# A pre-norm block with dilated local attention and an MLP: Wo's loads, a K halo and sums of h in another order, and seven products for all 18 pairs of W2 rows in group 5

## The chip, the cores and the metric

The kernel runs on one core of one Trainium2 chip. The metric is the device time of one execution in microseconds. Five engines run side by side, each in the order of its own instructions: TensorE (PE; its weight loads are shown as PEld), VectorE (DVE), ScalarE (ACT), GpSimd (POOL) and the SyncE queue (SP), which issues most of the DMAs.

## The reference

```python
h  = x + A(layernorm(x))        # x: 2048 rows of 576, bf16
h2 = h + B(layernorm(h))

def A(x):                       # 32 heads of 18, window 8, dilation 2
    q, k, v = split(x @ wqkv)   # wqkv: 576 x 1728
    idx = pos[:, None] - arange(8) * 2
    logits = einsum("bhsd,bhswd->bhsw", q, k[idx]) * 18 ** -0.5   # masked where idx < 0
    return einsum("bhsw,bhswd->bhsd", softmax(logits), v[idx]) @ wo

def B(x):
    y = layernorm(x)
    return gelu(y @ w1 + b1) @ w2 + b2      # w1: 576 x 4608, w2: 4608 x 576
```

## The kernel before

**Tiles and order.** The 2048 rows are 16 tiles of 128; tile j holds the rows 16 p + j, one per partition p. So the window of a row lies in the tiles j, j-2, ... of the same parity, and where it goes below tile 0 it comes from the partition before. K and V of the eight tiles of one parity lie in `kv_ring[j % 2]`. When a tile has been done, its own slot is loaded again from `kv_dram`, one partition shifted (`halo(j, 1)` for K, `halo(j, 2)` for V), for the tiles that follow. The attention goes through the tiles in `ATT_ORDER`, even ones from 14 down, then odd ones from 15 down, and the MLP in `GROUPS` of two: group 0 is tiles 14 and 12, group 4 is 15 and 13, group 5 is 11 and 9, group 6 is 7 and 5, group 7 is 3 and 1. All orders are written out by hand: each engine, the SP and POOL queues included, runs its instructions in the order of the program text.

**The QKV stage** has 24 visits of PE (two products of one tile each), with lists of what follows each visit: `after` for the other engines and `loads` for weight loads. A weight load is tied to the last evacuation before it (`pace`). The normed x of the odd tiles is turned by DMA: `out_x(i)` stores two tiles, `in_x(i)` reads them back transposed; `in_x(0)` serves the products from visit 12, `in_x(1)` those from visit 15, `in_x(2)` those from visit 18. `load_wo(qs)` issues two DMAs for each of four parts of Wo. Wo is first used in visit 17.

**The group stage.** For group k the loop runs MLP1 (four visits, v = 0 to 3; lists `m1[v]` are called ahead of each), in which ACT writes gelu into `h_all`, 36 blocks of F for the group's two tiles; after the visits 0 to 2 its first 24 blocks are there. Then comes MLP2 (`mlp2_fast` from group 2 on), and ahead of its products the visit of Wo for the two tiles c, d of group k+1. During this time DVE does the attention of the tiles e, f of group k+2 (`att_qk_one` is product, halo, sums; then `att_max`, `exps` on ACT, `att_den`), and in the next group's `m1[0]` `pv_sum` of both with `send_o` and `read_o`, which store o and read it back transposed into oT for Wo.

**Seven products.** In `mlp2_fast` two tiles of tokens, two blocks of F (a pair of W2 rows) and two halves of the columns make a 2 x 2 block product. 18 pairs m make up F. For pairs below `rows` it is done with seven products (`PRODUCTS`), which need four sums of h (`h_sums`, t = 0 to 3; s_slot gives their place) and four of W2 (`w2_sums`, t_slot; made once and kept). The pairs from `rows` on are done plainly with eight (`plain`). `rows` is 16 in the groups 2 to 5 and 18 in the groups of `FULL`, 6 and 7. Sum t=2 of h and t=2 of W2 are made in place, over a block that the seven products don't need. The sums of the pairs 0 to 11 lie in `kv_ring[0]`, those of 12 to 15 in rows of `q_all` or `x_all` that are free at that time. The hooks `x["hc"]`, `x["h"]`, `x["7"]`, `x["exp"]` and so on are called between the products, in the order of the list `steps`; h(c) and h(d) in the text are `ln2_h`, which adds Wo's product pw to x. `out1` ("o1") on DVE adds up the second tile's results, `reload_x` fetches x again for a later group, `out_sum` and `accumulate_hs` are DMAs of POOL that add into `x_all`.

Of the kernel before, what the change touches and what calls it, by code (L numbers as in the profile page):

```python
# [11 lines left out]
BF16 = mybir.dt.bfloat16  # L12
F32 = mybir.dt.float32
F16 = mybir.dt.float16
# [3 lines left out]
def kernel(  # L18
# [13 lines left out]
    P = 128  # L32
# [6 lines left out]
    KT = 5  # L39
# [5 lines left out]
    HALF = D // 2  # L45
# [10 lines left out]
    GROUPS = [ATT_ORDER[i:i + 2] for i in range(0, NT, 2)]  # L56
# [551 lines left out]
    def ring_blocks(r, b0, n, size):  # L608
        flat = kv_ring[r][:].rearrange("p w t d -> p (w t d)").bitcast(F16)
        return flat[:, b0:b0 + n * size].rearrange("p (m c) -> p m c", c=size)  # L610
# [5 lines left out]
    def t_slot(t, m0, m1):  # L616
        if t == 2:
            return w2_block(0, 1, m0, m1).bitcast(F16)
        i = (0, 1, None, 2)[t]
        if m0 >= 16:  # L620
            return ring_blocks(1, (2 * i + m0 - 16) * HALF, m1 - m0, HALF)
        if i == 2 and m0 < 16:
            return ring_blocks(0, RING_T + m0 * HALF, m1 - m0, HALF)
        part = 0 if m1 <= 8 else 1 if m1 <= 12 else 2
        rows, j0 = ((x_all, (1, 9, 13)[part]), (q_all, (4, 12, 0)[part]))[i]
        m = m0 - (0, 8, 12)[part]
        j = j0 + 2 * (m // 2)
        if m1 - m0 > 2:
            return rows[:, j:j + m1 - m0 - 1:2, :].bitcast(F16).rearrange("p a (b c) -> p a b c", c=HALF)
        return rows[:, j, (m % 2) * HALF:(m % 2 + m1 - m0) * HALF].bitcast(F16).rearrange("p (b c) -> p b c", c=HALF)  # L630

    SR = 12
    ring1_free = [False]
    step_of = [0]
    RING_T = 3 * SR * P

    def s_slot(t, m0, m1):
        if t == 2:
            return h_block(0, 1, m0, m1)
        i = (0, 1, None, 2)[t]  # L640
        if m0 < SR:
            return ring_blocks(0, (i * SR + m0) * P, m1 - m0, P)
        if not ring1_free[0]:
            rows, j = ((q_all, 15), (x_all, 10), (x_all, 8))[i] if step_of[0] == 2 else (q_all, 15 - 2 * i)
            return rows[:, j, (m0 - SR) * P:(m1 - SR) * P].bitcast(F16).rearrange("p (m c) -> p m c", c=P)
        return ring_blocks(1, 6 * HALF + (i * (NM - SR) + m0 - SR) * P, m1 - m0, P)

    def h_block(odd, i, m0, m1):
        return h_all[:, 2 * m0 + odd:2 * m1:2, i * P:(i + 1) * P].bitcast(F16)
# [49 lines left out]
    def c_(fn, *a):  # L699
        return lambda: fn(*a)  # L700
# [2 lines left out]
        return ap.rearrange("p (g c) -> p g c", g=2)  # L703

    def mlp2_fast(g, rows, tags, wo, hooks):
        last, summed = wo is None, rows < NM
        q, p, r, s = tags
        j0, j1 = g
        af = psum_pair(q, "po")
        a, f = (af[:, n, 0:HALF] for n in range(2))  # L710
        b, d = psum_pair(p, "po")[:, 0, 0:HALF], None
        o0, o1 = (new_o(j, summed) for j in g)
        flat = kv_ring[1][:].rearrange("p w t d -> p (w t d)")
        rest = halves(flat[:, W * 2 * D - 2 * D:W * 2 * D].bitcast(F32))
        bank = {1: a, 2: a, 3: f, 4: b, 6: b}

        def add(out, x, y):
            nc.vector.tensor_tensor(out=out, in0=x, in1=y, op=ALU.add)

        def last_out():  # L720
            nc.vector.tensor_copy(out=o0[:, HALF:HALF + HALF // 2], in_=f[:, 0:HALF // 2])
            nc.scalar.copy(out=o0[:, HALF + HALF // 2:D], in_=f[:, HALF // 2:HALF])
            nc.sync.dma_start(out=out3[:, j0, HALF:D], in_=o0[:, HALF:D])

        def out0(n0, n1):
            if summed:
                nc.scalar.copy(out=halves(o0), in_=af[:, :, 0:HALF])
                return
            add(halves(o0)[:, n0:n1], af[:, n0:n1, 0:HALF], halves(x_of(j0))[:, n0:n1])
            nc.sync.dma_start(out=out3[:, j0, n0 * HALF:n1 * HALF], in_=o0[:, n0 * HALF:n1 * HALF])  # L730

        def out1():
            if summed:
                add(o1[:, HALF:D], bank[5], o1[:, 0:HALF])
                add(o1[:, 0:HALF], b, o1[:, 0:HALF])
                out_sum(j1)
                return
            add(o1[:, 0:HALF], b, rest[:, 0])
            add(o1[:, HALF:D], bank[5], rest[:, 1])
            nc.sync.dma_start(out=out3[:, j1, :], in_=o1)  # L740

        def do_rest():
            if summed:
                nc.scalar.copy(out=o1[:, 0:HALF], in_=bank[7])
                return
            add(rest, bank[7].unsqueeze(1).to_broadcast([P, 2, HALF]), halves(x_of(j1)))

        def take():
            bank[7], bank[5] = (psum_pair(tag, "po")[:, 0, 0:HALF] for tag in (r, s))

        lo, hi, all_ = (0, SR), (SR, rows), (0, rows)
        seed = {"b": (1, 6), "d": (6, 5), "f": (5, 3)}
        does = {
            "wo": lambda: wo((r, s)), "e": take, "rest": do_rest, "o1": out1,
            "o0": lambda: last_out() if last else out0(0, 2), "lo": lambda: out0(0, 1),
            "11": lambda: plain(0, 0, a, rows), "12": lambda: plain(0, 1, f, rows),
            "21": lambda: plain(1, 0, b, rows), "22": lambda: plain(1, 1, bank[5], rows),
        }
        if rows < NM:
            steps = ["wo", "hc", (1, all_), "b", "h", "e", (7, lo), (2, all_), (6, all_), "6", "7", "d", "11", (7, hi), "rest", "in",  # L760
                      (5, all_), "f", "exp", (4, all_), "21", "22", "o1", "4", (3, all_), "12", "o0", "3"]
        elif not last:
            steps = ["wo", "hc", (1, all_), "b", "h", "e", (7, lo), (6, all_), "6", "d", "7", (2, all_), (7, hi), "rest", "in",
                     (5, all_), "f", (4, all_), "o1", "4", (3, all_), "o0"]
        else:
            steps = ["e", (1, lo), (7, lo), (1, hi), "b", "h", (7, hi), "rest", (6, all_), "d", (2, all_), "lo",
                     (5, all_), "f", (4, all_), "o1", (3, all_), "o0"]
        for step in steps:
            if isinstance(step, tuple):
                product(step[0], bank[step[0]], *step[1])  # L770
            elif step == "f" and last:
                add(f, bank[5], x_of(j0)[:, HALF:D])
            elif step in seed:
                nc.scalar.copy(out=bank[seed[step][1]], in_=bank[seed[step][0]])
            else:
                call([does[step]] if step in does else hooks.get(step, ()))
# [22 lines left out]
    with tc.manual_schedule(engines={ENG.PE, ENG.Activation, ENG.DVE, ENG.SP, ENG.Pool}):  # L799
# [129 lines left out]
            ln2_ins(c, d)  # L929

        loads = {}
        for v, fns in ((2, [(load_w1, 0)]), (3, [(load_w1, 1)]), (4, [(load_w1, 2)]), (6, [(load_wo, [0])]), (8, [(load_wo, [1, 2])]),
                       (11, [(load_wo, [3])]), (14, [(load_w1, 4)]), (18, [(load_w1, 5), (load_w2, 0)]), (19, [(load_w2, 1)]),
                       (20, [(load_w2, 2)]), (21, [(load_w2, 3)]), (22, [(load_w2, 4)])):
            loads[v] = [c_(*fn) for fn in fns]
        after = {
# [87 lines left out]
        def wo_visit(*duos, fill=False):  # L1024
            visit([wo_duo(j, tag) for j, tag in duos], (lambda: [ahead[0]() for _ in range(2)]) if fill else None)

        FULL = (6, 7)
        p, q, r, s = "ABDC"

        gelu_table()  # L1030
        for k, g in enumerate(GROUPS):
# [38 lines left out]
            if 2 < k < 7:  # L1070
                m1[0] += [c_(pv_sum, c), c_(send_o, c), c_(pv_sum, d), c_(read_o, c), c_(send_o, d), c_(read_o, d)]
            if k < 6:
                m1[1] = m1.get(1, []) + [c_(att_qk_one, e, 0)]
                m1.setdefault(3, [])
                if k == 2:
                    m1[0] += [c_(pv_sum, d), c_(send_o, d), c_(read_o, d)]
                    m1[3] += [c_(w2_sums, 0, 8, (2, 3)), c_(w2_sums, 8, 12, (2, 3)), c_(w2_sums, 12, 14, (0, 1)), c_(w2_sums, 14, 16, (0, 1)),
                              c_(w2_sums, 12, 14, (2, 3)), c_(w2_sums, 14, 16, (2, 3))]
                m1[3] += [c_(h_sums, 0, SR, (0,))]
                x["hc"] += [c_(h_sums, 0, SR, (2,))]  # L1080
                x["h"] += [c_(h_sums, 0, SR, (1, 3)), c_(h_sums, SR, 16)]
                x["7"] += [c_(att_max, [e]), c_(att_qk_one, f, 1), c_(att_max, [f])]
                x["exp"] += [c_(exps, e, f)]
                x["4"] += [c_(att_den, e, f)]
            else:
                if k == 6:
                    ring1_free[0] = True
                    m1[1].append(c_(w2_sums, 16, NM))
                m1[3] = m1.get(3, []) + [c_(h_sums, 0, SR)]
                if k == 7:  # L1090
                    mid[3] = {1: [c_(h_sums, SR, 16)]}
                    x["h"] += [c_(h_sums, 16, NM)]
            if k + 3 < len(GROUPS):
                x["3" if k == 2 else "in"] += [c_(reload_x, GROUPS[k + 3])]
            wo = None
            if c is not None:
                if k == 6:
# [51 lines left out]
```

## Time and profile before

| what | us |
|---|---|
| median of 3 runs (358.41 to 358.68) | 358.5 |
| the profiled execution | 358.75 |
| its span, first to last instruction | 357.0 |
| PE busy | 351.1 (98%) |
| PEld busy | 287.4 (81%) |
| DVE busy | 298.2 (84%) |
| ACT busy | 235.9 (66%) |
| POOL busy | 47.6 (13%) |
| granted TensorE clock | 1.0 |

The profile is of one execution, its times start at the first instruction, and durations that the prediction adds up come from it; 1.75 us of that execution lie outside the span. Busy times of PE include the pipelined part of each matmul, so that 98% doesn't mean PE at its peak. The trace also has the landing marks of each DMA, 16 for most (one for each of its rings), and each packet with its queue.

### The profile page before, as it was taken

Reading aid. Unit: us, or ns where it says so; the run is one execution under the profiler, and the core shown is the slowest. Engines: PE = TensorE matmul, PEld = TensorE weight load, DVE = VectorE, ACT = ScalarE, POOL = GpSimd, SP = SyncE. Lnnn points to the kernel's source line nnn. Section 1 sums busy time; section 2 is a strip of 40 time slices with the busy share of each in tenths; the row PEclk is TensorE's granted clock in tenths of the full one; section 3 lists DMA queues with packets and bytes.
Section 4 is the critical chain, followed back from the end, with each engine's and each line's share of the span. In section 5 each row is a group of like instructions: output and inputs, shape, how many; then the busy total and the mean of one; then the engine's idle time right before and its main releaser. Section 6 shows DMA issues by size and latency. Waiting matters only on the chain.

```text
span 357.0 us, 11587 instructions
## 1 busy us (share of the span) xinstructions
PE 351.1 (98%) x4945; PEld 287.4 (81%) x4945; DVE 298.2 (84%) x428; ACT 235.9 (66%) x524; POOL 47.6 (13%) x63
## 2 busy tenths in 40 slices
PE   8999999999999999999999999999999999999996
PEld 4787778887788877887788778877887788778874
DVE  5999999999988999999998999999999998520431
ACT  4889767996647692678567856695669566606620
POOL 2340004000212010201200220022002200210000
PEclk9999999999999999999999999999999999999999
DMA  7997799954847574942553445345535353262001
GB/s 244 327 292 188 174 249 291 388 195 89 207 72 119 162 230 76 129 75 69 92 101 75 117 104 79 86 109 108 85 85 101 66 87 50 59 129 38 4 1 34
DMA packets 63492, 46.29 MB, mean 130 GB/s; under 512 B 32192, under 2 KB 61760, under 8 KB 63440
## 3 DMA queue, kind: packets, MB, share of 16 engines
q1 hardware_dynamic: 59472, 41.50, 44.1%
q0 software_dynamic: 3744, 3.84, 10.3%
q8 instruction: 38, 0.62, 0.7%
q10 hardware_dynamic: 224, 0.22, 0.2%
q14 instruction: 14, 0.11, 0.1%
HBM read 23.38 MB, written 12.42 MB: 100 GB/s over the span
## 4 chain that ended last, share of the span: by engine, by line
DVE 43%; PE 43%; DMA 6%; issue 3%; ACT 2%; SPq 2%; POOL 0%; DVEq 0%; POOLq 0%; ACTq 0%
PE po L687 21%; PE pm L222 19%; DVE prod L401 7%; DVE prod L353 7%; DVE prod L344 6%; DVE prod L407 5%; DVE ln_stats L148 3%; PE pw L222 2%; DMA kv_ring<-kv_dram 2%; DVE h L467 1%; DMA x_all<-in_A_x_dram 1%; DVE den L395 1%; ACT h_all L578 1%; DVE q_all L408 1%; DMA td<-q_all 1%
## 5 line engine op out<-in xcount | busy, mean ns | idle before, releaser
L222 PE MATMUL pm<-hnT,w_sb 64*128 64x256 bf16 x2304 | 142.9, 269 | 0.0
L578 ACT ACTIVATE h_all<-pm,b_sb 128x256 f16<-128x256 f32 (+1 forms) x288 | 108.5, 497 | 50.8 <-PE pm L222 50.2
L222 PEld LDWEIGHTS <-w_sb 64*128 64x128 bf16 x2304 | 111.6, 94 | 15.1 <-issue 1.7
L222 PE MATMUL pq<-wq_sb,xnT 64*128 64x288 bf16 x720 | 54.9, 283 | 1.2 <-DMA xnT<-xd 0.6
L687 PEld LDWEIGHTS <-h_all 128*128 128x128 f16 x464 | 44.8, 98 | 12.9 <-issue 1.4
L222 PEld LDWEIGHTS <-xnT 64*128 64x128 bf16 x864 | 41.9, 94 | 12.4 <-DMA xnT<-xd 0.9
L353 DVE TENSOR_TENSOR prod<-prod 128x2304 bf16<-128x2304 bf16 (+1 forms) x64 | 44.2, 691 | 2.1
L401 DVE TENSOR_TENSOR prod<-kv_ring,probs 128x4608 bf16<-128x4608 bf16 x16 | 40.9, 2558 | 1.9 <-DMA kv_ring<-kv_dram 1.4
L344 DVE TENSOR_TENSOR prod<-kv_ring,q_all 128x4608 bf16<-128x4608 bf16 x16 | 40.9, 2555 | 0.2
L222 PE MATMUL pm<-hnT,w1h_sb 64*128 64x256 bf16 x288 | 39.2, 269 | 0.0
L407 DVE TENSOR_TENSOR prod<-prod 128x2304 bf16<-128x2304 bf16 (+1 forms) x32 | 33.9, 1058 | 1.1
L597 PEld LDWEIGHTS <-h_all 128*128 128x128 bf16 x288 | 27.8, 98 | 8.0 <-issue 1.2
L687 PE MATMUL po<-w2a_sb,h_all 128*128 128x288 bf16 (+1 forms) x252 | 34.0, 286 | 0.0
L687 PEld LDWEIGHTS <-kv_ring 128*128 128x128 f16 x252 | 24.7, 98 | 6.2
L597 PE MATMUL po<-w2a_sb,h_all 128*128 128x288 bf16 x224 | 28.6, 286 | 0.0
L787 POOL DMA_DIRECT2D x_all<-o_sb x12 | 10.7, 889 | 126.4 <-PE pw L222 54.4
L222 PE MATMUL pq<-wqh_sb,xnT 64*128 64x288 bf16 x144 | 27.4, 283 | 0.0
L492 POOL TENSOR_TENSOR ln_rstd<-ln_var,mhalf 128x1 f32<-128x1 f32 x13 | 9.8, 758 | 77.7 <-ACT ln_var L491 77.7
L667 DVE TENSOR_TENSOR kv_ring<-h_all 128x1536 f16<-128x1536 f16 (+3 forms) x9 | 6.8, 754 | 15.7 <-ACT h_all L578 15.7
L222 PE MATMUL pw<-wo_sb,oT 64*128 64x288 bf16 x256 | 19.5, 283 | 0.1
L161 POOL TENSOR_TENSOR ln_rstd<-ln_veps,mhalf 128x1 f32<-128x1 f32 (+2 forms) x14 | 13.1, 947 | 44.3 <-PE o_pt L182 26.4
L687 PE MATMUL po<-w2b_sb,h_all 128*128 128x288 bf16 (+1 forms) x112 | 18.8, 286 | 0.1
(121 smaller groups left out, 409.3 us busy)
## 6 DMA issues: line engine op xcount, KB each, us to landing
w_sb<-in_B_w_dram SPq DMA_DIRECT2D x6, 768.0 KB, 7.7
kv_ring<-kv_dram SPq DMA_DIRECT2D x28, 144.0 KB, 2.3
kv_dram<-kv_ring SPq DMA_DIRECT2D x13, 288.0 KB, 3.3
w2a_sb<-in_B_w_dram SPq DMA_DIRECT2D x3, 1008.0 KB, 10.2
x_all<-in_B_b_dram SPq DMA_DIRECT2D x15, 144.0 KB, 4.1
td<-q_all SPq DMA_DIRECT2D x14, 144.0 KB, 1.8
td<-hn SPq DMA_DIRECT2D x14, 144.0 KB, 1.8
x_all<-h POOLq DMA_DIRECT2D x14, 144.0 KB, 4.8
```

Source lines behind the costliest of these rows:

```text
L148: nc.vector.bn_stats(out=stats[:, i, c, :], in_=src[:, c * HALF:(c + 1) * HALF])
L161: nc.gpsimd.tensor_tensor(out=rstd[:], in0=veps[:], in1=mhalf[:].to_broadcast([P, n]), op=ALU.pow)
L222: last = nc.tensor.matmul(duo["g"][r ^ swap][i], lhsT=lhsT, rhs=rhs, start=(swap == 0 and i == 0 and kt == 0), stop=(swap == 1 and kt == K ...
L344: ins = nc.vector.tensor_tensor(out=prod[:], in0=k_ring[j % 2], in1=q_all[:, j, :].unsqueeze(1) .to_broadcast([P, W, D]), op=ALU.mult).ins
L353: nc.vector.tensor_tensor(out=prod[:, :, o * H:o * H + n], in0=prod[:, :, a * H:a * H + n], in1=prod[:, :, c * H:c * H + n], op=ALU.add)
L401: nc.vector.tensor_tensor(out=prod[:].rearrange("p w (d h) -> p w d h", h=H), in0=v_ring[j % 2].rearrange("p w (d h) -> p w d h", h=H), in ...
L407: nc.vector.tensor_tensor(out=prod[:, 0:n, :], in0=prod[:, 0:n, :], in1=prod[:, n:2 * n, :], op=ALU.add)
L492: ins = nc.gpsimd.tensor_tensor(out=rstd[:], in0=var[:], in1=mhalf[:], op=ALU.pow).ins
L578: pace[0] = nc.scalar.activation(out=hT(grp)[:, f, 0:N], in_=ps[:, r, i * N:(i + 1) * N], func=ACT.Gelu_apprx_tanh, bias=b1_sb[:, f:f + 1] ...
L597: nc.tensor.matmul(banks[half], lhsT=hT(grp)[:, f, i * P:(i + 1) * P], rhs=w2_rows(f)[:, half * HALF:(half + 1) * HALF], start=(f == 0), s ...
L687: nc.tensor.matmul(bank, lhsT=l, rhs=r, start=start, stop=stop, skip_group_check=True)
L787: nc.gpsimd.dma_start(out=x_of(j), in_=o_of.pop(j), accum_op=ALU.add)
```

## The change

- `load_wo`: parts 0 and 1 after visit 5 (before: 0 after visit 6, 1 and 2 after visit 8), parts 2 and 3 after visit 11 (before: 3).
- The K halo of tile e stands in `x["hc"]` rather than between `att_qk_a` and `att_qk_b` in `m1[1]`.
- From group 3 on, sum t=2 of h for the pairs 0 to 11 stands behind t=0 in `m1[3]`, ahead of h(c).
- Group 5 is in `FULL`: 18 pairs in seven products. For the pairs 16 and 17 it makes four sums of h and, in `x["h"]`, the sums 2 and 3 of W2; the sums 0 and 1 of W2 are made in group 3 ("exp"). They lie in rows 15, 13 and 11 of `q_all`. Before, group 6 made all four in `m1[1]`.
- The sums of h for the pairs 12 to 17 have other homes. Sum 1 of group 5 is in a new tile (`new_top`) in the place of hnT. Sums 0 and 3 of its pairs 16 and 17 are written into row 7 of `q_all`, over columns in which sum 3 of the pairs 12 to 15 was put before.
- `reload_x` of group 5 goes from the end of group 2 to that of group 3, and of group 6 from "in" of group 3 to the end of group 4.
- The output path of group 5 (`summed`) stays as it was.

```diff
         if m0 >= 16:
-            return ring_blocks(1, (2 * i + m0 - 16) * HALF, m1 - m0, HALF)
+            return q_all[:, 15 - 2 * i, (m0 - 16) * HALF:(m1 - 16) * HALF].bitcast(F16).rearrange("p (m c) -> p m c", c=HALF)
...
-    step_of = [0]
+    step_of, top = [0], [None]
+    homes = {2: ((q_all, 15), (x_all, 10), (x_all, 8)), 3: ((q_all, 11), (x_all, 10), (x_all, 8)),
+             4: ((q_all, 9), (x_all, 4), (x_all, 6)), 5: ((q_all, 9), (q_all, 5), (q_all, 7))}
...
         if not ring1_free[0]:
-            rows, j = ((q_all, 15), (x_all, 10), (x_all, 8))[i] if step_of[0] == 2 else (q_all, 15 - 2 * i)
-            return rows[:, j, (m0 - SR) * P:(m1 - SR) * P].bitcast(F16).rearrange("p (m c) -> p m c", c=P)
-        return ring_blocks(1, 6 * HALF + (i * (NM - SR) + m0 - SR) * P, m1 - m0, P)
+            if step_of[0] in FULL and t == 1:
+                rows, c = top[0][:].rearrange("p k c -> p (k c)"), 0
+            else:
+                rows, j = homes[step_of[0]][2 if m0 >= 16 else i]
+                rows, c = rows[:, j, :], (16 - SR - i) * P if m0 >= 16 else 0
+            return rows[:, (m0 - SR) * P - c:(m1 - SR) * P - c].bitcast(F16).rearrange("p (m c) -> p m c", c=P)
+        return ring_blocks(1, (i * (NM - SR) + m0 - SR) * P, m1 - m0, P)
+
+    def new_top():
+        top[0] = sb.tile([P, KT, 2 * P], BF16, tag="hnT", name="hnT")
...
-        last, summed = wo is None, rows < NM
+        last, summed = wo is None, g not in GROUPS[6:]
...
-        if rows < NM:
+        if summed:
...
-        for v, fns in ((2, [(load_w1, 0)]), (3, [(load_w1, 1)]), (4, [(load_w1, 2)]), (6, [(load_wo, [0])]), (8, [(load_wo, [1, 2])]),
-                       (11, [(load_wo, [3])]), (14, [(load_w1, 4)]), (18, [(load_w1, 5), (load_w2, 0)]), (19, [(load_w2, 1)]),
+        for v, fns in ((2, [(load_w1, 0)]), (3, [(load_w1, 1)]), (4, [(load_w1, 2)]), (5, [(load_wo, [0, 1])]),
+                       (11, [(load_wo, [2, 3])]), (14, [(load_w1, 4)]), (18, [(load_w1, 5), (load_w2, 0)]), (19, [(load_w2, 1)]),
...
-        FULL = (6, 7)
+        FULL = (5, 6, 7)
...
-                m1[1] = m1.get(1, []) + [c_(att_qk_one, e, 0)]
+                m1[1] = m1.get(1, []) + [c_(att_qk_a, e), c_(att_qk_b, e, 0)]
+                x["hc"] += [c_(halo, e, 1)]
...
-                m1[3] += [c_(h_sums, 0, SR, (0,))]
-                x["hc"] += [c_(h_sums, 0, SR, (2,))]
-                x["h"] += [c_(h_sums, 0, SR, (1, 3)), c_(h_sums, SR, 16)]
+                m1[3] += [c_(h_sums, 0, SR, (0,) if k == 2 else (0, 2))]
+                if k == 2:
+                    x["hc"] += [c_(h_sums, 0, SR, (2,))]
+                x["h"] += [c_(h_sums, 0, SR, (1, 3))]
+                if k in FULL:
+                    x["h"] += [new_top, c_(h_sums, SR, 16), c_(h_sums, 16, NM)] + [c_(w2_sums, 16, NM, (2, 3))] * (k == FULL[0])
+                else:
+                    x["h"] += [c_(h_sums, SR, 16)]
                 x["7"] += [c_(att_max, [e]), c_(att_qk_one, f, 1), c_(att_max, [f])]
+                if k == 3:
+                    x["exp"] += [c_(w2_sums, 16, NM, (0, 1))]
...
                 if k == 6:
                     ring1_free[0] = True
-                    m1[1].append(c_(w2_sums, 16, NM))
...
-            if k + 3 < len(GROUPS):
-                x["3" if k == 2 else "in"] += [c_(reload_x, GROUPS[k + 3])]
+            if k in (3, 4):
+                x["3"] += [c_(reload_x, GROUPS[k + 2])]
+            if k == 4:
+                x["in"] += [c_(reload_x, GROUPS[7])]
```

## Prediction

> **What bounds the kernel now.** I read the page's busy table and chain first, then the timelines of VectorE (DVE), TensorE (PE) and the SP queue around each place that the diff touches, then the landing marks and packets of the DMAs there.
>
> ```profile
> span 357.0 us, 11587 instructions
> PE 351.1 (98%) x4945; PEld 287.4 (81%) x4945; DVE 298.2 (84%) x428; ACT 235.9 (66%) x524; POOL 47.6 (13%) x63
> q8 instruction: 38, 0.62, 0.7%
> DVE 43%; PE 43%; DMA 6%; issue 3%; ACT 2%; SPq 2%; POOL 0%; DVEq 0%; POOLq 0%; ACTq 0%
> ```
>
> The q8 row gives packets, MB and a share of the DMA engines. PE lacks only 5.9 us of the span. The chain is DVE's until about 190 us and PE's after it. This is the place where it passes over, and the two MLP2 stages that can be compared (columns: start, duration, what):
>
> ```profile
> 188.80 3.68 DMA td<-q_all
> 192.53 2.91 DMA oT<-td
> 195.49 1.77 PE pw L222 x26
> ...
> 268.82 15.79 PE po L687 x128
> ...
> 304.60 15.54 PE po L687 x126
> ```
>
> 128 matmuls take 15.79 us and 126 take 15.54: 123 ns each. Group 5 is the second of these lines, group 6 (already on seven products) the third. Before 195.49 PE waits about 0.4 us for oT of tile 13. The only other stall of PE between 10 us and the tail is in the QKV stage, and DVE's waits late in the kernel are these (the bracket is idle time before the row and its releaser):
>
> ```profile
> 42.37 0.66 PE L222 MATMUL pq<-wq_sb,xnT 64*128 64x288 bf16 x8 [0.61 <-DMA xnT<-xd]
> ...
> 196.81 0.76 DVE L467 TENSOR_TENSOR h<-pw,x_all 128x576 f32<-128x576 f32 x1 [1.48 <-PE pw L222]
> ...
> 232.59 0.76 DVE L467 TENSOR_TENSOR h<-pw,x_all 128x576 f32<-128x576 f32 x1 [1.08 <-PE pw L222]
> 268.37 0.76 DVE L467 TENSOR_TENSOR h<-pw,x_all 128x576 f32<-128x576 f32 x1 [1.09 <-PE pw L222]
> 291.37 2.56 DVE L401 TENSOR_TENSOR prod<-kv_ring,probs 128x4608 bf16<-128x4608 bf16 x1 [0.63 <-DMA kv_ring<-kv_dram]
> ```
>
> So from group 3 on DVE has 1.1 to 1.5 us to spare per group of 35.8 us, all of it just before it reads pw.
>
> **Group 5's seven products.** 16 pairs in seven products and two pairs plain are 112 + 16 = 128 matmuls, 18 pairs in seven are 126: two fewer, 2 x 123 ns = **-0.25 us** of PE, as the rows of groups 5 and 6 differ. Its price is on DVE. Four more sums of 128x256 take 1.05 us (their starts at group 7: 341.48 to 342.21, and the last 0.28). Two W2 sums of 128x576 take 0.92 (rows of 0.45 to 0.47 us at 296.5 to 298.3). That is 1.97 us in "h". Moving sum t=2 ahead of h(c) takes 0.87 out of that place: t=0 starts at 266.40, t=2 would end at 268.2, and h(c) starts at 268.37 anyway, so the idle 1.09 us hides it. Net, DVE reaches att_max(e) at 275.0 instead of 273.9: **1.1 us later**. PE is not kept waiting by the sums: starting at 268.75, products 1, 7 (12 pairs), 2 and 6 hold it until 268.75 + (18+12+18+18) x 0.123 = 276.9, and the last sum is needed only there. If that cover of 1.9 us were gone, the shortfall would be paid one for one. The ACT copy "d" has 6 matmuls (0.74 us) for cover where it had 8; it ended 0.59 us after product 6 (276.10 to 276.69). out1 comes at 283.4 and frees its bank at 283.8; MLP1 of group 6 reaches that bank 1.1 us after 284.3. Reads of the new hnT tile by product 6 end at 276.9, and the transposes of LN2 into that slot were issued at 278.79, so they don't wait either.
>
> **Group 3, group 4, group 6.** In group 3 the two W2 sums (0.92) stand where t=2 (0.87) has left: even. In group 4 t=2 moves into the idle 1.08 us and nothing is added; DVE then waits for bank 5 at out1 (it was at 246.47, PE done at 246.2): 0 to -0.1. In group 6 four W2 sums (1.8 us at 296.5) go; DVE waited afterwards for ACT (0.40) and PE (1.74), so nothing.
>
> **What the 1.1 us meet.** In group 6 DVE makes o of tiles 3 and 1, which Wo needs. Tile 1's transpose landed at 301.40 and its first weight load was at 302.72: 1.3 us of slack, 1.07 after PE's gain. Of DVE's 1.1, 0.63 falls away if the halo it waited for is on time. That halo (issued 288.09) landed on 15 rings at 289.91 to 290.20, on the last at 291.28: 9 of its 144 packets ran after a 16 KB packet of q8 at 288.84 to 289.80. PE's 9,890 instructions over 38 such packets are 260 each: they are PE's code. The halo would now start a microsecond later, behind that packet. So tile 1 is about 0.5 late, lands near 301.9 and is needed at 302.48: cost 0 unless a transfer is hit. The next code packet was at 301.15, while the transpose would move at 300.4 to 301.5. A hit costs what it cost elsewhere: the transpose of tile 3 took 4.08 us from issue (292.74) to landing against 2.8, so 303.2 and a stall of 0.7; the store of tile 13 took 3.7 against 1.7, 2.0 more than usual. I take 0 as likeliest, and 0 to 1.4 as bounds.
>
> **Wo's loads.** Now parts [1, 2] lie on SP ahead of the second transpose of x (issued 36.82, landed 40.71 to 42.32, the last ring behind a code packet at 40.06): that is PE's 0.61 us. Moved to visit 11 they free SP of 1.9 us there, and that stall should go. But [0, 1] now go out near 22.9 us, behind load_w1(2), which landed between 25.90 and 28.74 (three rings late), and ahead of halo and store of x that landed at 29.31 and 30.30. On the late rings two parts are 20 KB, about 1.0 us at the 74 ns per 1.5 KB of load_w1. The first transpose waits for that store; it landed at 34.76 and PE's first load of it was at 34.82, no slack. Against the added 1.0 stand a code packet (30.92 to 32.04) and the Wo packets behind it, which it would escape: 0.3 to 0.6. So PE loses 0.2 to 0.9 at 34.8 and gains 0.61 at 42.4: -0.4 to +0.3, I take -0.1.
>
> By the Trainium skill (DMA: Bandwidth & Descriptors, Queues, rings and completion order) descriptors of one ring are consumed in order, so bytes queued earlier delay all that follow on that ring; the trace agrees, since the K store issued at 20.68 landed last at 26.85 and load_w1(2) behind it at 28.74.
>
> Four DMAs instead of two ahead of the third transpose (44.10, landed 47.64, needed near 50.1) cost it about 1.0 of 2.4 us slack: nothing. None of this moves DVE, which runs without a gap over 0.8 us from 24 to 195; PE gets what it gained at 42 only as far as oT of tile 13 allows. That store (188.80) landed at 192.48 with 18 packets behind a code packet of 189.27 to 191.04. If PE is earlier, so is that packet, and the store is hit less. At 195 I take **-0.1**, bounds +0.1 and -1.0.
>
> **Halo, reloads.** From group 3 on nothing else of SP stands between the halo's old and new place; in group 2 two output stores go first (1.4 us) and the halo is needed 14 us later. reload_x of group 5 and 6 now waits for product 3 with SP behind it, as it did in group 2 (173.10 to 176.85, next SP work 180.46): SP is free near 214 and 250, next needed at 216.5 and 252.3. All nothing; without that cover the K and V halos would be late, about 2 us each.
>
> **The sum.** -0.25 - 0.1 + 0 = -0.35 us on a profiled execution of 358.75 us (span 357.0 and 1.75 around it). The median of the runs is 358.5, 0.25 below it; I apply the difference to the median: 358.15, written 358.2. A measurement of this kernel can tell about 0.2% (0.72 us) from no change, and this is half of it.
>
> **Rivals.**
> 1. *The QKV stall goes whole, and oT of tile 13 comes in time.* For it: PE has no other stall until 195, and a shift of 0.6 brings the code packet to 188.7, mostly ahead of the store at 189.2. Against it: no slack at 34.82. It gives 0.61 + 0.4 + 0.25 = 1.26: 357.2. Chance 0.22.
> 2. *Slower: oT of tile 1 comes late in group 6.* The code packet near 301 hits the transpose, which DVE's delay has brought to it. It decides from the point where tile 1 lands after 302.48, 1.1 us later than now. For it: packet and transpose would overlap by half a microsecond. Against it: code packets are 172 to 392 instructions apart, so that the place is uncertain by more than that. A stall of 0.7 to 1.4 less 0.25 gives 358.9 to 359.7. Chance 0.23.
> 3. *The matmuls are saved but the copies and sums around them are waited for* ("d" with 0.74 us of cover, sums with 1.9). Then 0.25 is given back: 358.5. Chance 0.1.
>
> The forecast keeps 0.45. By the Trainium skill (Runtime: NRT & Kernel Launch, Instruction fetch mechanics) the sequencer fetches its next 256 instructions by its own DMA queue and the crossing is mostly hidden; by that alone rival 2 would cost nothing. The trace disagrees in part: PE never waits for code, but the fetches delay other transfers, as at 189.27 and 288.84.
>
> **Range and chances.** 357.2 (rival 1) to 359.3 (rival 2 short of its worst) leaves out about 0.2. Faster by over 0.2% is rival 1 and a tail of the forecast: 0.28. Slower by over 0.2% is the upper half of rival 2 and things unseen: 0.18. Within: 0.54. The forecast's own range is 357.7 to 358.6.
>
> **What would show it.** After: group 5's L687 rows number 126 in about 15.5 us with no idle time; no [.. DMA xnT<-xd] row near 42, perhaps one at 35; 128x256 sums in group 5 and att_max at +1.1 us; in group 6 no halo wait at 291, and no wait of PE for oT<-td near 302.5. A PE wait there over 0.9 us, or one over 0.7 at 35 that lives on past 195, makes the forecast wrong; a first PE pw after tile 13 before 194.8 makes rival 1 right.

## The result and the profile after

| kernel | median us | lowest to highest | runs |
|---|---|---|---|
| before | 358.54 | 358.17 to 359.00 | 9 |
| after | 359.59 | 358.99 to 360.91 | 9 |

The changed kernel is 1.05 us slower: ratio 1.0028, 95% interval 1.0019 to 1.0038. The forecast was 358.2 with a range of 357.2 to 359.3, so the result lies 0.3 us above the range and on the other side of no change. Rival 2 had named the place and 358.9 to 359.7.

The profiled execution of after is one of 359.59 us. These four lines of its page answer to those of before:

```profile
span 357.8 us, 11596 instructions
PE 351.9 (98%) x4943; PEld 291.4 (81%) x4943; DVE 298.9 (84%) x432; ACT 235.7 (66%) x524; POOL 47.4 (13%) x63
q8 instruction: 38, 0.62, 0.8%
PE 68%; DVE 21%; DMA 4%; ACT 3%; SPq 1%; issue 1%; POOL 0%; POOLq 0%; DVEq 0%; ACTq 0%
```

Two matmuls are gone (4945 to 4943), DVE has four instructions more, and the span grew by 0.8 us. Busy times say nothing here: DVE gained 0.7 us of 298. The timeline of PE does, around Wo of group 6 (start, duration, what, in brackets the idle time before and its releaser):

```profile
302.16 0.65 PE L222 MATMUL pw<-wo_sb,oT 64*128 64x288 bf16 x8
302.65 0.29 PE L222 MATMUL pw<-woh_sb,oT 64*128 64x288 bf16 x2
303.65 0.66 PE L222 MATMUL pw<-wo_sb,oT 64*128 64x288 bf16 x8 [0.71 <-ACT h_all L578]
```

In the kernel before, the same rows were:

```profile
302.23 0.65 PE L222 MATMUL pw<-wo_sb,oT 64*128 64x288 bf16 x8
302.72 0.29 PE L222 MATMUL pw<-woh_sb,oT 64*128 64x288 bf16 x2
302.85 0.65 PE L222 MATMUL pw<-wo_sb,oT 64*128 64x288 bf16 x8
```

The matmuls of tile 3 begin 0.07 us earlier than before, those of tile 1 0.80 later. The span's 0.8 us is made between these rows. (The medians differ by 1.05 us; no profile shows the other 0.2.) The last row of after names ACT, whose work had long been done. The weight-load row of the same moment names the DMA:

```profile
303.65 1.46 PEld L222 LDWEIGHTS <-oT 64*128 64x128 bf16 x26 [1.02 <-DMA oT<-td]
```

That is the one to believe, since the transpose of tile 1 landed at 303.48 to 303.61. Before, it had landed at 301.25 to 301.40.

Why it came late is read backwards on DVE, from group 5:

```profile
256.26 2.56 DVE L401 TENSOR_TENSOR prod<-kv_ring,probs 128x4608 bf16<-128x4608 bf16 x1 [1.21 <-DMA kv_ring<-kv_dram]
...
268.60 0.96 DVE L676 TENSOR_TENSOR h_all<-h_all 128x1536 f16<-128x1536 f16 x1
269.48 1.42 DVE L467 TENSOR_TENSOR h<-pw,x_all 128x576 f32<-128x576 f32 x2
...
275.30 0.44 DVE L666 TENSOR_TENSOR q_all<-w2b_sb,q_all 128x576 f16<-128x576 bf16 x1
275.67 0.44 DVE L666 TENSOR_TENSOR w2b_sb<-w2b_sb 128x576 f16<-128x576 bf16 x1
276.04 0.59 DVE L368 TENSOR_REDUCE peak<-logits 128x32 f32<-128x256 f32 x1
...
292.86 2.56 DVE L401 TENSOR_TENSOR prod<-kv_ring,probs 128x4608 bf16<-128x4608 bf16 x1
```

att_max(e) of group 5 comes at 276.04, before it was 273.90: 2.14 us, not the 1.1 forecast. The forecast's 1.1 is in it: from h(c) to att_max it takes 6.56 us instead of 5.53, with the six new sums at 274.32 to 276.04 and t=2 gone from there. The other 1.1 us, by which h(c) is late, begins with the first row, a wait of 1.21 for the V halo. The kernel before had no wait there:

```profile
254.97 2.56 DVE L401 TENSOR_TENSOR prod<-kv_ring,probs 128x4608 bf16<-128x4608 bf16 x1
```

There, DVE had 1.09 us of idle time ahead of h(c) (268.37). In after, t=2 (the row at 268.60) stands in it, so that the halo's wait goes through and h(c) starts at 269.48 with no idle time left.

The issue and the landing marks show the rest. SP sent the transpose of tile 1 at 300.38, before at 298.62 (SP timeline of after, then of before):

```profile
300.38 2.13 SPq L439 DMA_TRANSPOSE oT<-td  x1
```

```profile
298.62 1.21 SPq L439 DMA_TRANSPOSE oT<-td  x1
```

In after its data packets ran from 301.69 to 303.01, 33 ns each on average, beside and behind a 16 KB code packet of PE at 300.97 to 302.08, and the issue itself took 2.13 us instead of 1.21. Before, they ran from 299.92 to 300.95, 19 ns each, and the code packet began at 301.15, after them.

### The profile page after: what moved, and what is told of

Same layout as the page of the kernel before. It is cut to its first block, busy times and chain, and to the rows that moved or that the text cites. A ratio compares the mean times of both kernels' runs of the same rounds, so it can differ in the third digit from the quotient of the medians.

```text
span 357.8 us, 11596 instructions
## 1 busy us (share of the span) xinstructions
PE 351.9 (98%) x4943; PEld 291.4 (81%) x4943; DVE 298.9 (84%) x432; ACT 235.7 (66%) x524; POOL 47.4 (13%) x63
## 3 DMA queue, kind: packets, MB, share of 16 engines
q0 software_dynamic: 3744, 3.84, 10.0%
## 4 chain that ended last, share of the span: by engine, by line
PE 68%; DVE 21%; DMA 4%; ACT 3%; SPq 1%; issue 1%; POOL 0%; POOLq 0%; DVEq 0%; ACTq 0%
PE pm L222 34%; PE po L696 25%; PE po L597 5%; DVE prod L353 4%; PE pw L222 4%; DVE prod L344 4%; DVE ln_stats L148 3%; DVE prod L401 3%; ACT h_all L578 2%; DVE prod L407 2%; DMA x_all<-in_A_x_dram 1%; DMA kv_ring<-kv_dram 1%; DMA hnT<-td 1%; SPq L104 1%; DVE ln_mv L149 1%
## 5 line engine op out<-in xcount | busy, mean ns | idle before, releaser
L222 PEld LDWEIGHTS <-w_sb 64*128 64x128 bf16 x2304 | 113.4, 94 | 13.5 <-issue 1.4
L696 PEld LDWEIGHTS <-h_all 128*128 128x128 f16 x456 | 43.9, 98 | 13.0 <-issue 1.4
L222 PEld LDWEIGHTS <-xnT 64*128 64x128 bf16 x864 | 43.4, 94 | 10.4 <-DMA xnT<-xd 0.9
L783 ACT COPY po<-po 128x288 f32<-128x288 f32 x17 | 6.5, 385 | 17.1 <-PE po L696 17.1
```

The lines of the kernel that those rows point to most:

```text
L222: last = nc.tensor.matmul(duo["g"][r ^ swap][i], lhsT=lhsT, rhs=rhs, start=(swap == 0 and i == 0 and kt == 0), stop=(swap == 1 and kt == K ...
L696: nc.tensor.matmul(bank, lhsT=l, rhs=r, start=start, stop=stop, skip_group_check=True)
```

## The experiments

All times are medians beside runs of the kernel before on the same chip. The ratio and its interval come from the runs and can differ a little from the quotient of the medians. Three theories stood at the start: D, the six sums make tile 1 late; W, Wo's order costs it; P, the other placings do.

| label | what | us | before there | ratio, interval |
|---|---|---|---|---|
| e1_g5_plain | after, group 5 without seven products for pairs 16, 17 | 359.17 | 358.51 | 1.0018, 1.0007 to 1.0028 |
| e2_wo_only | before + Wo's order | 358.71 | 358.51 | 1.0003, 0.9994 to 1.0012 |
| e3_no_sums | after without the six sums | 358.64 | 358.51 | 1.0008, 0.9997 to 1.0019 |
| e4_more_dve | before + 1.0 us of DVE work | 359.19 | 358.51 | 1.0018, 1.0010 to 1.0027 |
| e5_reload_later | after, reloads later | 359.08 | 358.36 | 1.0021, 1.0009 to 1.0033 |
| e6_g5_plain_reload_later | e1, reloads later | 358.83 | 358.36 | 1.0017, 1.0004 to 1.0030 |
| e7_reload_only | before, reloads moved | 358.50 | 358.36 | 0.9995, 0.9987 to 1.0004 |
| e8_spread | after, reloads later, W2 sums spread | 358.26 | 358.36 | 0.9995, 0.9986 to 1.0003 |
| e9_homes_reload | before + homes and reloads | 358.64 | 358.53 | 0.9999, 0.9990 to 1.0008 |
| e10_homes_reload_dve | e9 + 1.0 us of DVE work | 359.12 | 358.53 | 1.0018, 1.0009 to 1.0027 |
| e11_dve_code_later | e4, 28 PE instructions fewer at the start | 358.97 | 358.53 | 1.0011, 1.0001 to 1.0022 |
| e12_spread_old_wo | e8, Wo's order of before | 358.48 | 358.53 | 0.9996, 0.9987 to 1.0005 |
| e13_t2_back | after, t=2 back behind h(c) | 359.49 | 358.53 | 1.0024, 1.0014 to 1.0035 |
| e14_spread_reload_early | e8 with the change's reloads | 359.75 | 358.53 | 1.0035, 1.0022 to 1.0048 |
| e15_g5_plain_less | e6, t=2 and K halo back too | 358.88 | 358.53 | 1.0013, 1.0004 to 1.0022 |

### Wo's order, the sums, and DVE work alone

```diff
 e1:  FULL = (6, 7)          # w2_sums(16, NM, (2, 3)) in m1[1] of group 6
 e2:  only the table `loads`
 e3:  products 3 to 7 of pairs 16, 17 take the operands of pairs 14, 15 in group 5
-  x["h"] += [new_top, c_(h_sums, SR, 16), c_(h_sums, 16, NM)] + ...
+  x["h"] += [new_top, c_(h_sums, SR, 16)]     # w2_sums(16, NM, (2, 3)) in m1[1] of group 6
 e4 (before):
+  if k == 5: x["h"] += [c_(more_sums, 1)]     # two sums of 128x256, one of 128x576
```

> The changed kernel with group 5 back on 16 pairs in seven products and two plain; all else of the change stays (Wo's loads, K halo, sum t=2 ahead of h(c), homes, reloads, two W2 sums in group 3; the other two go back to group 6). Theory D (DVE's six more sums in group 5 make o of tiles 3 and 1 late, and PE waits for oT of tile 1 in group 6): the wait of 1.0 us is gone, 358.5 +- 0.3. Theory W (the order of Wo's loads costs the time) and theory P (the other placings, halo, sum t=2, reloads, cost it): 359.6, as with the whole change.

> The kernel before with the new order of Wo's loads alone. Theory D: PE loses about 0.6 us at visit 12 (near 35 us) and no longer 0.61 at 42, DVE's chain to 195 us is as before: 358.5 +- 0.3. Theory W: 359.3 to 359.6. Theory P: 358.5.

> The changed kernel in which group 5 runs its 126 matmuls without the sums of the pairs 16 and 17: their products 3 to 7 take the operands of the pairs 14 and 15, which leaves those two pairs' share of the result out; the W2 sums t=2 and 3 are made in group 6. Theory D: no wait for oT of tile 1, and PE's 0.25 us remain: 358.2 to 358.5. Theories W and P: 359.6.

> The kernel before with about 1.0 us of additional DVE work at the end of x['h'] of group 5 (two sums of 128x256 and one of 128x576 into row 9 of q_all, which nothing reads), PE's instructions as before. Theory D: half of the loss or more without any other part of the change, since tile 1's oT had 1.3 us of slack in the profile before and less when a halo is hit: 358.7 to 359.3. Theories W and P: 358.5 +- 0.2.

W falls: e2 is not told from the kernel before. D holds: e4 changes nothing but DVE's work and has the same stall in the same place (timeline of PE in e4):

```profile
303.52 0.66 PE L222 MATMUL pw<-wo_sb,oT 64*128 64x288 bf16 x8 [0.80 <-DMA oT<-td]
```

e3 has no such row and gives back 0.9 us of the 1.05; at 358.64 it is still above its 358.2 to 358.5. But e1, with neither sums nor saved matmuls, should have been 358.5 and was 359.17. Its profile shows a halo wait of 1.29 us at 256.84, and PE waiting at 273 for the copy "b". So P was not done with.

### The reloads

```diff
 e5 (after), e6 (e1):
-  if k in (3, 4): x["3"] += [c_(reload_x, GROUPS[k + 2])]
+  if k in (4, 5): m1[0] += [c_(reload_x, GROUPS[k + 1])]     # behind read_o(d)
 e7 (before):
-  x["3" if k == 2 else "in"] += [c_(reload_x, GROUPS[k + 3])]
+  if k in (3, 4): x["3"] += [c_(reload_x, GROUPS[k + 2])]    # group 7 stays in "in" of group 4
 e9 (before): as e7, and the change's homes of groups 3 and 4
```

> The changed kernel, but x of groups 5 and 6 is read again behind the transposes of o in m1[0] of the next group (groups 4 and 5), not at the end of groups 3 and 4. Theory R: in the changed kernel the reload of group 6 (issued 248.46, 279 KB moved until 251.8, 9 packets held behind a code packet until 253.2) lies on the rings just ahead of the V halo that is issued at 252.40; 135 of that halo's packets ran by 254.46 and 9 only from 255.43, so DVE waited 1.21 us at 256.26, and its idle time ahead of h(c), which would have taken that up, was spent on t=2. By R that wait goes here, att_max(e) of group 5 comes at 275.0 and not 276.0, PE's wait for oT of tile 1 at 303 shrinks to 0 to 0.3 us: 358.5 to 358.9 us. Theory D (the six sums alone make tile 1 late; the reload doesn't matter): the wait at 256 stays or its going changes nothing, 359.3 to 359.6.

> e1_g5_plain with the same later reloads. e1 had no sums in group 5 and was still 0.66 us over the kernel before, with a halo wait of 1.29 at 256.84 and a stall of PE at 273 behind the ACT copy 'b'. Theory R: both go, 358.4 to 358.6, the kernel before. If the surplus of e1 comes from sum t=2 ahead of h(c) or from the K halo's place instead, it stays at 359.0 to 359.2.

> The kernel before, with nothing changed but the place of the reloads of groups 5 and 6 (as in the change: end of group 3 and end of group 4). Theory R: DVE has the wait for the V halo at 256 (1.0 to 1.3 us) which the kernel before doesn't have; its idle time ahead of h(c) at 268, 1.09 us there, is gone and takes it up, so that the time hardly moves: 358.4 to 358.8. If the wait doesn't come, the reload isn't its cause, and 358.5 as well; the two are told apart by the rows at 256 and 268.

> The kernel before, with the change's homes for the sums of groups 3 and 4 (rows of q_all and x_all) and its reloads of x. e7 moved the reloads alone, but there nothing made them wait for product 3, they were issued at 245.5 instead of 248.5, and the row at 256 could not be tested. Theory R: here they are issued at 248 to 249, DVE gets the wait of about 1.2 us for the V halo at 256, and the idle time ahead of h(c) at 268 (1.09 us before) takes it up: 358.4 to 358.7 us, no wait of PE at 303. If the halo comes on time (no wait over 0.3 at 256), the reload is not the cause of that wait.

e7 could not show it: nothing in it made the reload wait, so it was issued about 3 us earlier than in the change. e9 did. The SP queues at that place, of e9 and then of the kernel before:

```profile
244.98 1.04 SPq L462 DMA_DIRECT2D x_all<-in_A_x_dram  x2
...
248.58 0.81 SPq L462 DMA_DIRECT2D x_all<-in_A_x_dram  x2
252.51 0.33 SPq L339 DMA_DIRECT2D kv_ring<-kv_dram  x1
```

```profile
244.76 1.05 SPq L462 DMA_DIRECT2D x_all<-in_A_x_dram  x2
252.29 0.33 SPq L339 DMA_DIRECT2D kv_ring<-kv_dram  x1
```

The rows at 244.98 and 244.76 are the reload of group 7, which both have. In e9 the reload of group 6 follows it and goes out 3.9 us ahead of the halo, and the halo landed at 254.64 to 256.52 instead of 254.02 to 254.69. In after the packets tell why (queue q0 is POOL's, q1 SP's, q8 PE's code):

```
before 249.17-253.98 q0 432 packets     after 249.27-255.44 q0 432 packets
                                              249.44-251.78 q1 279 packets (reload)
       250.89-251.79 q8 1 packet              251.47-252.36 q8 1 packet
                                              252.34-253.24 q1 9 packets (rest of the reload)
       253.25-254.36 q1 144 packets (halo)    253.74-254.46 q1 135 packets (halo)
                                              255.43-256.64 q1 297 packets (9 of the halo, a store of o)
```

The same code packet that harmed nothing before now holds the last 9 packets of the reload on one DMA engine, and on that engine POOL's sums and the last 9 packets of the halo come a microsecond or more late. All 17 profiles fit: the seven kernels whose reload waits for product 3 and goes out at 248 to 249 (after, e1, e3, e9, e10, e13, e14) have a wait of 1.2 to 1.5 us at 256, the other ten have none over 0.04.

And e9 costs nothing (0.9999): its rows of DVE show the wait, and that the idle time ahead of h(c) has gone:

```profile
256.61 2.56 DVE L401 TENSOR_TENSOR prod<-kv_ring,probs 128x4608 bf16<-128x4608 bf16 x1 [1.46 <-DMA kv_ring<-kv_dram]
...
268.86 0.73 DVE L467 TENSOR_TENSOR h<-pw,x_all 128x576 f32<-128x576 f32 x1
```

e5 has no wait at 256, as theory R said, but missed in time: 359.08 rather than 358.5 to 358.9. Without the reload's wait the six sums still cost 0.7 us, as the added work in e4 did. (Its profiled execution was its slowest, 361.11 us, with a wait of 1.52 at 84.8 that no other kernel has; its rows are used here only from 197 us on.) e6 was expected at the kernel before and is 0.47 over it.

### Both together, and a spread

```diff
 e8 (e5):
-  x["h"] += ... + [c_(w2_sums, 16, NM, (2, 3))] * (k == FULL[0])
+  k == 4: x["exp"] += [c_(w2_sums, 16, NM, (3,))]
+  k == 5: m1[3] = [c_(w2_sums, 16, NM, (2,))] + m1[3]
 e10: e9 + e4          e12: e8, `loads` as before, homes index 1 for m0 >= 16
 e14: e8, reload_x of groups 5 and 6 in x["3"] as in the change
 e13 (after):
-  m1[3] += [c_(h_sums, 0, SR, (0,) if k == 2 else (0, 2))]
+  m1[3] += [c_(h_sums, 0, SR, (0,))];  x["hc"] += [c_(h_sums, 0, SR, (2,))]
```

> The changed kernel with the later reloads of e5, and the two W2 sums of pairs 16 and 17 taken out of 'h' of group 5: sum 3 stands in 'exp' of group 4, where DVE waited 0.73 us for ACT, sum 2 in m1[3] of group 5 ahead of h(c). Theories R and D together: DVE reaches att_max(e) of group 5 0.3 to 0.5 us later than in the kernel before, no wait of PE at 303, and the two matmuls saved are left: 358.1 to 358.4. By D alone without R (the reload does not matter) 358.7 to 359.0.

> e9 with the 1.0 us of DVE work in 'h' of group 5 that e4 had. If lost idle time and added work simply add on DVE, as in the changed kernel: e9's wait leaves no idle ahead of h(c), the work is then the changed kernel's 1.1 us, oT of tile 1 lands near 303 to 303.6: 359.1 to 359.8, with a wait of PE at 303. If e4's 0.7 us was all there is (a code packet that hits the transpose, whatever the lateness), 359.1 to 359.3. The DVE rows at 256, 268 and 292 and the landing of tile 1 tell them apart rather than the time.

> e8 (later reloads, W2 sum 3 made in group 4 and sum 2 ahead of h(c)) with Wo's loads in the order of before, and the sums 0 and 3 of h for the pairs 16 and 17 in row 5 of q_all. A try at a kernel that beats both: e8 gave 358.26 beside 358.36, e2 (Wo order alone) 0.1 to 0.2 over before. If both add: 357.9 to 358.2. If DVE is too late for tile 1 at 301 again: 358.6 to 359.

> The changed kernel with sum t=2 of h (pairs 0 to 11) of groups 3 to 5 behind h(c) again, as before. In the changed kernel t=2 (0.87 us) stands in the time in which DVE waited for pw (1.09 us before), and the halo wait of 1.21 at 256 came on top. Theory I (the idle time ahead of h(c) takes up either t=2 or the halo's wait, not both): here it takes up the wait, t=2 then costs its 0.87 behind h(c), att_max(e) of group 5 comes at 276.0 as in the changed kernel: 359.2 to 359.7, unchanged. Theory T (moving t=2 is itself what makes PE wait, since ln2 and the copy 'b' come later): 358.6 to 358.9.

> e8 (358.26 beside 358.36) with the reloads where the change has them. e9 had those reloads and homes alone and a halo wait of 1.46 us at 256, and was no slower (358.64 beside 358.53), with the idle time of 1.09 us ahead of h(c) to take it up. Here t=2 and W2 sum 2 stand in that time. Theory I: the wait comes, nothing takes it up, tile 1 is 1.0 to 1.3 us later than in e8, its transpose meets the code packet of 301: 358.9 to 359.3 with a wait of PE near 303. If the reload costs nothing here either: 358.2 to 358.5.

e14 against e8 and e9 is the test that settles it, though at 359.75 it lies above the 358.9 to 359.3 that theory I gave. The same reload costs 0.11 us where DVE's idle time is free (e9 less its before) and 1.32 where t=2 and a W2 sum stand in that time (e14's +1.22 less e8's -0.10). DVE and PE in e14:

```profile
255.86 2.56 DVE L401 TENSOR_TENSOR prod<-kv_ring,probs 128x4608 bf16<-128x4608 bf16 x1 [1.31 <-DMA kv_ring<-kv_dram]
...
269.45 1.42 DVE L467 TENSOR_TENSOR h<-pw,x_all 128x576 f32<-128x576 f32 x2
```

```profile
272.59 1.88 PE L696 MATMUL po<-w2a_sb,h_all 128*128 128x288 bf16 x14 [0.39 <-ACT po L783]
303.83 0.67 PE L222 MATMUL pw<-wo_sb,oT 64*128 64x288 bf16 x8 [0.92 <-DMA oT<-td]
```

It pays twice, and theory I had only the second: h(c) comes late and with it, on ACT, the copy "b" (0.39), and tile 1 comes late (0.92). In e8, without the early reload, h(c) stands at 268.08 with 126 matmuls in group 5, and PE waits for nothing between 50 and 340.

e13 says that the move of t=2 alone neither costs nor gains here: the idle time takes up either t=2 or the halo's wait. att_max(e) stood at 275.79 there, 276.04 in after. e10 shows the same: counted from the first matmul of group 5's MLP2, att_max comes after 6.10 us in e10 and 6.05 in e4 (5.15 before). The halo's wait has gone into the idle time, the added work is left, and the time is that of e4, 0.6 to 0.7 over before.

e8 and e12 were tries at beating both kernels. They beat the change by about 1 us, but neither can be told from the kernel before.

### The code packet

```diff
 e11 (e4), warm-up of PE at the start:
-  for n in [512] * 8 + [P] * 8:          for n in range(12):  P columns
+  for n in [512] * 10:                   for n in range(4):   3 * P columns
```

> e4 (before + 1.0 us of DVE work in group 5, 359.19, tile 1's transpose landed on 15 rings by 301.9 and on the last at 303.47, behind a code packet of 301.48 to 302.42), with PE's warm-up matmuls at the start merged into fewer of the same total columns: 28 PE instructions less, so that every later code packet comes 0.8 to 1.0 us later in PE's work. Theory C (the price of the lateness is the hit by that packet): the packet comes at 302.3, the transpose lands by 302.0, PE's wait at 303.5 (0.80) shrinks to 0 to 0.3: 358.4 to 358.8. If lateness itself costs, whatever the packets: 359.1 to 359.3. A hit elsewhere in the chain (the V halo at 290) would bring the wait back; the rows show it.

e11 is no clean test, and my idea of what sets the packet's place fell with it: 28 instructions less did not bring it later in PE's work. It came at 300.91, 0.65 us ahead of tile 3's first pw (301.56), in e4 0.46 ahead (301.94). The stall at 303 is gone in its profile all the same (an execution of 358.06 us), with the packet 2.62 us behind the transpose's issue instead of 2.50; its median lies between both theories (358.97). What bears on the packet is a table over all 17 profiles, in the order of how far ahead of tile 3's first pw the transpose was issued (that counts its lateness against PE's own progress):

| kernel | transpose issued | ahead of tile 3's first pw | code packet | behind the issue | landed, first to last mark | last mark after issue | PE waits for oT |
|---|---|---|---|---|---|---|---|
| e7 | 297.84 | 4.16 | 300.61 to 301.83 | 2.77 | 300.52 to 300.67 | 2.83 | no |
| e9 | 298.54 | 3.91 | 301.44 to 302.40 | 2.90 | 301.21 to 301.37 | 2.83 | no |
| e2 | 298.33 | 3.89 | 300.91 to 302.09 | 2.58 | 301.02 to 301.18 | 2.85 | no |
| e1 | 299.39 | 3.84 | 302.00 to 303.10 | 2.61 | 302.04 to 302.19 | 2.80 | no |
| e15 | 298.32 | 3.76 | 300.68 to 301.66 | 2.36 | 300.86 to 301.02 | 2.70 | no |
| e12 | 298.28 | 3.73 | 300.57 to 301.76 | 2.29 | 300.95 to 301.12 | 2.84 | no |
| e6 | 298.52 | 3.71 | 300.82 to 301.77 | 2.30 | 301.16 to 301.34 | 2.82 | no |
| before | 298.62 | 3.61 | 301.15 to 302.35 | 2.53 | 301.25 to 301.40 | 2.78 | no |
| e8 | 297.95 | 3.54 | 300.49 to 301.65 | 2.54 | 300.66 to 300.80 | 2.85 | no |
| e3 | 299.00 | 3.53 | 301.31 to 302.58 | 2.31 | 301.75 to 301.90 | 2.90 | no |
| e10 | 299.08 | 3.38 | 301.16 to 302.31 | 2.08 | 301.73 to 303.40 | 4.32 | 0.20 |
| e11 | 298.29 | 3.26 | 300.91 to 301.94 | 2.62 | 301.00 to 301.15 | 2.86 | no |
| e5 | 300.85 | 3.00 | 303.10 to 304.09 | 2.25 | 303.46 to 305.14 | 4.29 | 0.56 |
| e4 | 298.98 | 2.96 | 301.48 to 302.42 | 2.50 | 301.80 to 303.47 | 4.49 | 0.80 |
| e14 | 299.37 | 2.77 | 301.77 to 302.71 | 2.40 | 302.10 to 303.79 | 4.42 | 0.92 |
| e13 | 299.93 | 2.06 | 301.16 to 302.11 | 1.23 | 303.50 to 303.62 | 3.69 | 0.90 |
| after | 300.38 | 1.78 | 300.97 to 302.08 | 0.59 | 303.48 to 303.61 | 3.23 | 0.71 |

Down to e3 the transpose goes out 3.53 us or more ahead of that pw, takes 2.7 to 2.9 us and harms nothing. Of the seven kernels below, in which it goes out later against PE, six have it landing 0.4 to 1.7 us later than usual and PE waiting; e11 has not. No start of the packet by itself divides them: it began 2.08 to 2.50 us behind the issue in e10, e5, e14 and e4, which were hit, but 2.29 to 2.36 us behind it in e12, e6, e3 and e15, which were not. What divides them is what was left to move. The transpose has 640 data packets and 32 of 4 bytes. In each of the six that were hit, at least two of the small ones ran only when the code packet had ended (in e4 one data packet too, in e14 two); in the eleven others none did, although in e3, e6 and e12 4 to 15 data packets ran beside the code packet. This fits a code packet that holds one DMA engine, and a hit if that engine still has a part of the transpose; the records do not name the engine.

So the lateness at which PE is hit can be smaller than the slack: e4's transpose, 0.36 us later than the one before, would have landed at 301.8 without the packet, well before PE's need at 302.56 (0.62 behind tile 3's first pw, as before). The same sum has e5, e10 and e14 in time without it. After's, 1.76 later, would have landed at 303.2 and been late by about 0.4 in any case, e13's by about 0.1. That the packet is the cause in each of these rows is argued from the times; no run moved the packet alone.

### What is left

```diff
 e15 (e6), t=2 as in e13, and:
-  m1[1] = m1.get(1, []) + [c_(att_qk_a, e), c_(att_qk_b, e, 0)];  x["hc"] += [c_(halo, e, 1)]
+  m1[1] = m1.get(1, []) + [c_(att_qk_one, e, 0)]
```

> e6 (no sums of pairs 16 and 17 in group 5, later reloads; 358.83 beside 358.36) with t=2 and the K halo in their places of before as well. What is left of the change is Wo's order, the homes and two of the W2 sums in group 3. If t=2 or the K halo made e6's surplus of 0.47: 358.4 to 358.6. If Wo's order or the homes did: 358.8 to 359.0.

t=2 and the K halo are not the source of e6's surplus: e15 still has +0.35. What it keeps of the change is Wo's order, the homes, two W2 sums in group 3 and reloads in a place of their own.

One stretch of the profiles leaves out all that happens before 195 us: from PE's first MLP2 matmul of group 3 (197.19 before) to that of group 6 (304.53).

| kernel | that stretch, us |
|---|---|
| before, e2, e6, e7, e9, e11 | 107.35 |
| e8, e12 | 107.10 |
| e3 | 107.26 |
| e15, e10, e1 | 107.69, 107.73, 107.76 |
| e5, after | 107.84, 108.07 |
| e4, e13, e14 | 108.32, 108.46, 108.74 |

The two matmuls saved are the 0.25 us of e8 and e12. The early reload with its homes (e9) and Wo's order alone (e2) cost nothing here, and e6 is as the kernel before, so its surplus of 0.47 does not lie in this stretch. e15's 0.34 does: its weight loads have a wait of 0.48 for an oT at 231.11 that the kernel before has not. Wo's order alone gave +0.2 in the medians (e2, not told from zero), and taking it back in e12 gave nothing. What makes the 0.2 to 0.4 us of e6 and e15 stays open.

## Why the prediction was wrong, step by step

**Group 5's seven products.** Right: where nothing else was late (e8, e12) the two matmuls were worth 0.25 us. In after the MLP2 stage went from 268.75 to 284.54 (15.79) to 268.85 to 284.47 (15.62), 0.17 us less. The rows of the six sums took 1.72 us where 1.97 was forecast, 1.9 with the time that they put ahead of the first of them, and PE shows no wait for them or for "d". Rival 3 did not come.

**What the 1.1 us meet.** This step failed, and with it the forecast. It took 0 as likeliest, with tile 1 about 0.5 us late against 1.07 of slack. The transpose of tile 1 went out 1.76 us late, since att_max was 2.14 us late and not 1.1; that alone would have cost PE about 0.4 us. Beside the code packet it then took 3.23 us from issue to landing instead of 2.78, and PE's stall was 0.80 to 0.88 us. The step's own words named the packet near 301, the transpose and a stall of 0.7 to 1.4, and rival 2 held against them that the packet's place was uncertain. It did not see how little room there was: in the kernel before the packet begins 0.2 us behind the last data of the transpose (300.95), and of the seven kernels whose transpose goes out later against PE six met it. The spread of 172 to 392 instructions was too wide a doubt: over the 17 profiles the packet came 0.4 to 1.4 us ahead of tile 3's first pw (1.08 before, 1.19 after). But these 1.1 us are still more than the 0.36 us that were enough in e4, so that a hit stays in part a matter of chance. The credit of 0.63 for the halo at 291 was real (no wait at 292.86).

By the Trainium skill (Runtime: NRT & Kernel Launch, Instruction fetch mechanics) the crossing of a code block is mostly hidden; the prediction had noted that by this alone rival 2 would cost nothing. The runs bear that out for PE, whose only idle time in after between 197 and 310 us is the one for oT, and not for others' transfers: e4 has 1.7 us more for the transpose beside such a packet, and 0.7 us more for the kernel.

**Halo, reloads.** This step failed too: "all nothing". It looked at SP, which was free, and not at the rings, where 288 KB of the reload now lie just ahead of the halo. Its cost was a DVE wait of 1.21 us. The step had named late K and V halos, at about 2 us each, for the case that the SP queue's cover was gone; that cover was there, and the V halo alone came late.

**One cover, used twice.** Behind both lies the term for t=2: "the idle 1.09 us hides it". That is true, and it spends the time which had taken up late halos. Each edit was set against the idle time by itself, and the sum of 0.87 and 1.21 against 1.09 was never made. In numbers: h(c) 1.11 late, and 1.03 more from h(c) to att_max(e) (the sums' 1.9 less t=2's 0.87), are the 2.14 by which att_max(e) was late.

**Wo's loads.** Right in kind: the stall at 42 went, and one of 0.34 (weight loads) came at 35.45. The -0.1 did not come: the first po stands at 197.28 against 197.19 before, 0.09 later. Not foreseen was a wait at 50.4, where in_x(2) landed at 50.36. PE reached tile 15's pw at 194.99 instead of 194.60, and nearly all of that is gone at 197, since in the kernel before PE then waited for oT of tile 13 and in after it did not. Rival 1 fell at the point that the text had put against it.

## What to carry to other kernels

Idle time of an engine off the critical path is a buffer: before an edit is booked as hidden in it, add up everything that the same edit list puts there, late transfers included, and see what follows when the buffer is empty. A DMA that is moved has two covers, the queue that issues it and the rings that carry it; look at whose packets are on the rings in the 4 us behind its new issue. Where a transfer's data ends just ahead of a code packet, its slack can be the gap to that packet rather than the slack to its consumer.

## What the runs showed of the hardware that was not expected

- A transposing DMA beside a 16 KB code packet can land 0.4 to 1.7 us later (3.2 to 4.5 us between issue and last mark instead of 2.7 to 2.9). In e4, e5, e10 and e14 15 marks were on time and the last came 1.5 us behind them; in e3, e6 and e12 the two overlapped as well, and nothing was late.
- One late ring is enough: 9 of a halo's 144 packets ran 1 us behind the others, and DVE waited 1.2 us for them.
- The code packet near 301 kept its place in PE's work within 1.1 us over 17 profiles (0.4 to 1.4 us ahead of tile 3's first pw), also where 28 PE instructions were taken away at the start.
